# Full-width inverse steps, 33 weight columns, crossed decay sums and a new order in a fused RWKV-7 and SoLU kernel

## The chip, the cores and the metric

The kernel runs on one core of a Trainium2 chip. A core has five engines that run side by side, each its own instructions in order: TensorE (PE in the profile; its weight loads stand apart as PEld), VectorE (DVE), ScalarE (ACT), GpSimd (POOL) and SyncE (SP). SP, POOL and ACT also issue DMAs, which move data between DRAM and the on-chip memories. An instruction that needs another engine's result waits on a semaphore. The metric is the time of one execution on the device, in microseconds (us), as the median over several runs.

## What is computed

The first half is a recurrence with a 40 x 40 state for each of 4 batches and 8 heads over 768 steps; the second is a layer with a softmax gate and a norm over its outputs.

```python
for t in range(S):                      # S = 768, batch B = 4, heads H = 8, D = 40
    y[:, :, t] = einsum('bhd,bhde->bhe', r_t, state)
    Sa = einsum('bhde,bhe->bhd', state, a_t)
    state = state * w_t[:, :, None, :] - einsum('bhd,bhe->bhde', Sa, b_t) \
            + einsum('bhd,bhe->bhde', v_t, k_t)
x = y.transpose(0, 2, 1, 3).reshape(B * S, H * D)      # 3072 x 320
h = x @ w_in                                           # 320 x 1024
sm = softmax(h);  solu = h * sm
ln = (solu - mean) / sqrt(var + 1e-6) * g_ln
out = ln @ w_out                                       # 1024 x 320
```

All arithmetic is fp32. `w_in` and `w_out` lie in DRAM as float64; their words are taken apart on the chip and turned into fp32 ("narrowed").

## The kernel before

**Chunks.** The recurrence is cut into chunks of C = 64 steps. A chunk works on two of the four batches, one on partitions 0 to 63 and one on 64 to 127, so there are N = 24 chunks: even and odd ones alternate between the two batch pairs. Inside a chunk all is matrix products: `logged` takes the logarithm of w, a product with a triangle of ones sums it (`decay`, or `decay_by_halves` for chunks 12 to 23), the exponentials scale a and b (`aT`, `kb`), and the products of a with b give a strictly triangular 64 x 64 matrix for each head and batch (`norm`, kept negated as `nt`). The chunk's answer needs the inverse of one minus that matrix.

**The inverse.** Each 64 x 64 matrix is cut into 32 x 32 blocks (Q = 32). The two diagonal blocks of two chunks (one group n, 12 groups) are written to DRAM by `norm_stored`, read back by `spread` with one small matrix per partition (twice, the upper 64 partitions doing the other half of the columns), and inverted by forward substitution on VectorE (`invert`, lines 543 to 564): step j multiplies row j's factors into the columns done so far and adds. A step with fewer than four columns takes one fused instruction a column (L552); the others are cut into two parts, both products first (L560), then both sums (L563). The result goes to DRAM (`unloaded`) and comes back with `bring`: `tu` gets the block for the first 32 steps, `uh` that for the last 32. `flip` transposes the first; `couple` multiplies `nt`'s off-diagonal block with it, ScalarE brings the product to `wy` (L602), `close` multiplies that with `uh`, and ScalarE puts the result into the last columns of `tu` (L614). In `wy` the columns 32 to 63 hold an identity, so that close's product also copies `uh` itself into place; the factor `hi` zeroes the rows of the first 32 steps.

**The chunk's end.** `scores_k`, `scores_v`, `carried` and `driven` build the right side in `px`, ScalarE copies it to `x0`, `solved` multiplies with `tu`, `read` forms the answers, `answered` scales them, and `leave` and `left` turn them through DRAM into rows `xT` of the second half. Two chunks later (LAG = 2) `hidden` multiplies with `w_in` (five parts, H in the order), `highest`, `exped`, `weighed`, `spreadof` and `powered` do gate and norm, `folded` transposes, and `products_of` multiplies with `w_out`. The front of a chunk (loads, decays, `norm`) runs five chunks ahead (AHEAD = 5).

**Matmuls.** An fp32 matmul appears as two instructions in the trace. Operands of 64 rows and 64 columns use one quadrant of the array, so that four such products can run side by side; `in_turn` deals the units of work out over the quadrants.

**The order.** Every piece of work has a name: `i3.7` is step 7 of inverse 3, `Tc5` the decay sums of chunk 5 on PE and `xe5`, `xi5` their exponentials, `lg` the logarithm, `N`, `nt` the norm product and its copy, `sn` its way to DRAM, `Z`, `B`, `U` the clearing, loading and unloading of an inverse, `tu`, `uh` the loads of `bring`, `F`, `C`, `wy`, `D`, `tl` flip to close with their copies, `V`, `S`, `R0`, `R1` driven, solved and read, `nb`, `ns`, `nf` the three stages of narrowing a weight matrix part, and so on. The loops at the end of the function list the pieces in a default order; then all pieces named in the text `ORDER` (lines 31 to 74) come first, in the order written there, and the rest follow in the default order. Each engine and each DMA queue runs its pieces in that order and waits in line for what is not there yet. `ORDER` reaches to chunk 10; from there on the default loop sets the order: in it an h product group (`run(6)`) stands ahead of `couple`, another (`run(7)`) between `couple` and `close`.

## Time and profile before

| | |
|---|---|
| runs shown | 533.07, 534.18, 534.34 us; median 534.18 |
| the profiled execution | 535.16 us, of which 533.3 us are the span from the first to the last instruction |
| granted TensorE clock over the span | 0.99 |
| busy share of the span | PE 91%, PEld 74%, DVE 79%, ACT 59%, POOL 34% |
| the chain of work that ended last | PE 77%, DMA 8%, DVE 7%, ACT 3%, SP's queue 3%, issue 2% |
| `couple` (py<-tu,nt), 64 weight columns | 768 matmuls of 64x32, mean 223 ns each |
| `close` (py<-uh,wy), 64 weight columns | 768 matmuls of 64x32, mean 223 ns each |
| inverse steps on DVE | 576 products and 576 sums, mean 204 ns each; 144 fused ones, mean 242 ns |
| decay sums by halves (pst<-lw,cst) | 96 matmuls of 64x160, mean 309 ns each |

The profile is one execution, seen by the hardware profiler. "Busy" is the time in which an engine has an instruction in work; since instructions overlap in their pipelines, the mean duration of one is longer than the distance from one to the next. Times in a timeline or a chain are the start in us from the span's start, then the length. An instruction is named by engine, line (L552), operation and tiles (output<-inputs); "x12" is a count. The chain of waits follows the work back from the last instruction to what released it. A line that serves many callers (L318 is the matmul helper) is told apart by its tiles.

### The profile page before, as it was taken

What the parts mean: (1) busy time and instruction counts of PE and PEld (TensorE: products, weight loads), DVE (VectorE), ACT (ScalarE), POOL (GpSimd) and SP (SyncE); (2) the same over time, 40 slices, a digit from 0 to 9 for tenths busy, and PEclk for the clock granted to TensorE, in tenths of its full rate; (3) what the DMA queues carried; (4) which work ended last, traced back from release to release, by engine and by line L of the source; (5) the groups of instructions that cost most, each with busy time, mean ns of one, the idle gap of its engine ahead of it and who ended that gap; (6) DMA issues with size and microseconds to landing.
All of it is one profiled execution on the core that took longest, in us unless ns stands there. A gap on an engine that the chain in (4) does not pass through costs nothing.

```text
span 533.3 us, 28056 instructions
## 1 busy us (share of the span) xinstructions
PE 487.6 (91%) x12029; PEld 394.7 (74%) x12029; DVE 420.0 (79%) x1800; ACT 313.1 (59%) x627; POOL 180.2 (34%) x328
## 2 busy tenths in 40 slices
PE   4457589898999999999999999999999999999997
PEld 3345476666888877877888788788778877887766
DVE  5589988998998988879789879879979888544322
ACT  3546457785856655745766665566556655664433
POOL 3543237224434242533053343334252421210300
PEclk9999988998999999999999999999999999999999
DMA  9997679846666778766266675676554551420210
GB/s 155 171 185 149 150 140 187 189 95 118 133 134 129 131 154 142 150 142 141 48 135 117 124 163 100 116 152 123 105 120 95 109 115 43 103 68 27 62 53 25
DMA packets 194475, 63.95 MB, mean 120 GB/s; under 512 B 166840, under 2 KB 186528, under 8 KB 194352
## 3 DMA queue, kind: packets, MB, share of 16 engines
...
## 4 chain that ended last, share of the span: by engine, by line
PE 77%; DMA 8%; DVE 7%; ACT 3%; SPq 3%; issue 2%; DVEq 0%; ACTq 0%
PE po L318 19%; PE h L318 18%; PE py L318 6%; PE pyo L318 6%; PE px L318 6%; PE ps L318 4%; PE pu L318 3%; DMA a<-in_a_dram 3%; PE plnT L883 2%; PE pkv L435 2%; PE psr L318 2%; PE pb L435 2%; PE pa L435 2%; SPq L344 2%; DVE prod L560 1%
## 5 line engine op out<-in xcount | busy, mean ns | idle before, releaser
L318 PE MATMUL h<-w_in,xT 64*64 64x512 f32 (+1 forms) x1064 | 122.2, 551 | 0.4 <-issue 0.2
L318 PE MATMUL po<-w,lnT 128*128 128x160 f32 x768 | 114.7, 304 | 0.0
L318 PEld LDWEIGHTS po<-w,lnT 128*128 128x128 f32 x768 | 105.4, 190 | 4.6 <-issue 0.8
L560 DVE TENSOR_TENSOR prod<-blk,uu 128x48 f32<-128x48 f32 (+19 forms) x576 | 93.9, 204 | 1.2
L563 DVE TENSOR_TENSOR uu<-uu,prod 128x48 f32<-128x48 f32 (+19 forms) x576 | 94.2, 204 | 0.0
L525 POOL DMA_DIRECT2D nt_dram<-nt x86 | 50.1, 590 | 110.9 <-ACT nt L513 109.6
L318 PEld LDWEIGHTS h<-w_in,xT 64*64 64x64 f32 x1064 | 38.9, 133 | 24.9 <-issue 20.6
L834 DVE TENSOR_REDUCE nmax<-h 128x1 f32<-128x1024 f32 x24 | 29.3, 1221 | 32.1 <-PE h L318 31.5
L871 POOL TENSOR_TENSOR rs<-var,mhalf 128x1 f32<-128x1 f32 x24 | 13.7, 571 | 119.4 <-ACT var L863 119.1
L344 POOL DMA_DIRECT2D raw_r<-in_r_dram x48 | 33.0, 692 | 26.5 <-ACT r L379 24.5
L862 ACT ACTIVATE sq<-e,mu 128x1024 f32<-128x1024 f32 x24 | 26.9, 1120 | 19.9 <-DVE e L850 19.9
L479 DVE TENSOR_TENSOR lu<-pu,cst 128x512 f32<-128x512 f32 x24 | 16.5, 687 | 27.0 <-PE pu L318 27.0
L842 ACT ACTIVATE e<-h,nmax 128x1024 f32<-128x1024 f32 x24 | 26.7, 1110 | 17.5 <-DVE nmax L834 17.3
L850 DVE SCALAR_TENSOR_TENSOR e<-h,e 128x1024 f32<-128x1024 f32 x24 | 29.3, 1221 | 5.4 <-ACT e L842 5.2
L602 ACT ACTIVATE wy<-py,cst 128x256 f32<-128x256 f32 x24 | 11.4, 474 | 37.4 <-PE py L318 37.4
...
L552 DVE SCALAR_TENSOR_TENSOR uu<-blk,uu 128x30 f32<-128x30 f32 (+3 forms) x144 | 26.9, 242 | 2.5 <-DMA blk<-nt_dram 1.9
L665 ACT COPY st<-psr 128x416 f32<-128x416 f32 (+1 forms) x44 | 14.2, 377 | 24.7 <-PE psr L318 24.7
L629 ACT COPY kvT<-pkv 104x1024 f32<-104x1024 f32 x24 | 24.2, 1010 | 6.7 <-PE pkv L435 6.4
L318 PEld LDWEIGHTS py<-tu,nt 64*64 64x64 f32 x768 | 16.3, 141 | 14.2 <-issue 7.6
L318 PE MATMUL pu<-x,tu 64*64 64x104 f32 x768 | 25.9, 265 | 0.7 <-ACT bT L445 0.5
L318 PE MATMUL px<-lv,psi 64*64 64x104 f32 x768 | 24.2, 264 | 2.2 <-DVE lv L479 2.2
...
## 6 DMA issues: line engine op xcount, KB each, us to landing
...
```

Source lines behind the costliest of these rows:

```text
L318: nc.tensor.matmul(o, lhsT=lhsT, rhs=rhs, start=start, stop=stop, skip_group_check=True)
L344: queue.dma_start(out=x[half(p), :, 0:D], in_=ap[2 * bp + p, :, ci * C:(ci + 1) * C, :].rearrange("h t d -> t h d"))
L435: nc.tensor.transpose(out=t[0:W2, p, at + C * j:at + C * j + C], in_=x[half(p), 2 * j:2 * j + 2].rearrange("p a b -> p (a b)")[:, skip:ski ...
L525: queue.dma_start(out=blocks[n][e].rearrange("(a x h) s c -> a x s h c", a=GRP, x=2)[at, x], in_=nt[home:home + Q].rearrange("p h j c -> p ...
L552: nc.vector.scalar_tensor_tensor(out=u[:, c, j + 1:Q], in0=nb[:, j, j + 1:Q], scalar=u[:, c, j:j + 1], in1=u[:, c, j + 1:Q], op0=ALU.mult, ...
L560: nc.vector.tensor_tensor(out=ts[-1], in0=nb[:, j:j + 1, j + 1:Q].to_broadcast([P, hi - lo, m]), in1=u[:, lo:hi, j:j + 1].to_broadcast([P, ...
L563: nc.vector.tensor_tensor(out=u[:, lo:hi, j + 1:Q], in0=u[:, lo:hi, j + 1:Q], in1=x, op=ALU.add)
L629: return lambda: nc.scalar.copy(out=o[0:W2].rearrange("p b j t -> p b (j t)"), in_=t[0:W2])
L834: nc.vector.tensor_reduce(out=nmax, in_=d["h"], axis=AX.X, op=ALU.max, negate=True)
L842: nc.scalar.activation(out=e, in_=d["h"], func=AF.Exp, bias=d["nmax"], accum_out=d["esum"])
L850: nc.vector.scalar_tensor_tensor(out=d["e"], in0=d["h"], scalar=1.0 / DFF, in1=d["e"], op0=ALU.mult, op1=ALU.mult, accum_out=d["mu"])
L862: nc.scalar.activation(out=pair("A" if i == N - 2 else "h", "sq").rearrange("p a b -> p (a b)"), in_=d["e"], func=AF.Square, scale=-float( ...
```

## The change

1. **Full-width steps.** For the first six inverses (`WIDE = 6`) a step with one column stays one fused instruction; every other step becomes one product over all its columns and one sum. Each is a piece of its own: the product keeps the name `i3.7`, the sum is `j3.7`, so other work can be put between them. Inverses 6 to 11 keep the old steps.
2. **33 weight columns.** `couple` uses the last 33 of `nt`'s 64 columns as weights, `close` 33 rows and 33 columns of `wy`. The first of the 33 meets a row of zeros. `wy` has 33 columns, the last of them zero; the identity and the factor `hi` leave the constants table. The block that the identity used to copy now comes by two DMAs of its own (`ut`, on SP) into `tu`, and `uh` holds half as many heads. The copies to `wy` and into `tu` are two ScalarE instructions each, one for each half of the partitions.
3. **Crossed decay sums.** From chunk index 12 (the 13th chunk) on, `logged` writes the second half of the heads' logarithms to the other 64 partitions, in three instructions in place of one, and the four products of `decay_by_halves` lie on four quadrants of the array in place of two.
4. **Order.** `ORDER` is new throughout and reaches to chunk 12. In the default loop `couple` stands ahead of the h group of `run(6)`.
5. The load of `g_ln` moves from ScalarE's queue to GpSimd's.

```diff
@@ -24,53 +24,72 @@
 LAG = 2
 EARLY = 10
 NK = 5
+NARROW = Q + 1
+WIDE = 6
 FIRST = 6
+CROSSED = EARLY + 2
 SPLITS = {2: (0, 0, 0, 2, 4), 24: (0, 0, 0, 0, 2)}
-w0 b0 b1 w1 a0 lg0 Tc0 xi0 xe0 Tei0 sb0 Tb0 Ta0 L1 lg1 Tc1 Eei0 Ea0 v0 Eb0 xi1 xe1 N0 nt0 Tei1 Eei1 sb1 Tb1 a1 Ta1 Ea1
-L0 Eb1 N1 nt1 w2 lg2 a2 Tc2 nb0 k0 Z0 sn0 nb1 ns1 nf1 sn1q sk0 ns0 nf0 sn1 w3 xe2 b2 Z1 Ta2 xi2 B0 Tei2 Eei2 r0 Ea2
...
+w0 b0 b1 lg0 Tc0 xi0 xe0 sb0 w1 K1 lg1 Tc1 xi1 sb1 Tei0 a0 Eei0 Ta0 Ea0 L0 a1 w2 Tb0 xe1 Tei1 Eb0 N0 k0 k1 sk0 nt0 Tb1
+Ta1 k2 b2 Eei1 Ea1 Eb1 N1 Z0 nb0 L1 lg2 nt1 r0 cr0 Tc2 xe2 Tei2 xi2 sb2 nb1 ns1 nf1 sk1 b3 sk2 sn0 sn1q sn1 w3 lg3 Tb2
+B0 i0.1 Tc3 Eei2 xi3 i0.2 b4 b5 i0.3 a2 xe3 j0.3 i0.4 j0.4 i0.5 j0.5 i0.6 j0.6 i0.7 j0.7 Eb2 g Ta2 Ea2 N2 i0.8 j0.8
+i0.9 j0.9 i0.10 ns0 Z1 v0 r1 sb3 j0.10 i0.11 j0.11 w4 lg4 Tc4 a3 nt2 a4 i0.12 j0.12 i0.13 w5 Tei3 Eei3 j0.13 i0.14
...
 """
 LN_EXP = "natural_log_exp_and_others"
@@ -84,8 +103,6 @@
         ident=np.eye(P),
         cum=same & (s <= t),
         tri=row < np.arange(C)[None, :],
-        eye_hi=row == Q + np.arange(Q)[None, :],
-        hi=(row >= Q).astype(np.float64),
         mean=np.full((P, P), 2.0 ** -10),
     )
     at, where = 0, {}
@@ -173,11 +190,10 @@
     r_t = zeroed(nc.gpsimd, "r", [P, H, C], 1, pad)
     st_t = zeroed(nc.vector, "st", [P, 2, 8, C], NPAIR)
     tu_t = zeroed(nc.vector, "tu", [P, H, 3 * Q], 2)
-    uh_t = zeroed(nc.vector, "uh", [P, 2 * H, Q], 2)
+    uh_t = zeroed(nc.vector, "uh", [P, H, Q], 2)
     x0 = const.tile([P, 2, 4, W2], FP32, name="x0")
-    wy = const.tile([P, 2, 4, C], FP32, name="wy")
-    nc.vector.tensor_copy(out=wy.rearrange("p h j c -> p (h j) c")[:, :, Q:],
-                          in_=c_("eye_hi").unsqueeze(1).to_broadcast([P, 8, Q]))
+    wy = const.tile([P, 2, 4, NARROW], FP32, name="wy")
+    nc.vector.memset(wy[:, :, :, Q:], 0.0)
     above = const.tile([C, Q // 2, Q], FP32, name="above")
     nc.gpsimd.memset(above, 1.0)
     for x in range(Q // 2):
@@ -381,7 +397,13 @@
     def logged(i):
         lw = st[i]["lw"] = two.tile([P, DM], FP32, tag="lw", name="lw", bufs=1)
-        nc.scalar.activation(out=lw, in_=st[i]["raw_w"].rearrange("p h d -> p (h d)"), func=AF.Ln)
+        raw = st[i]["raw_w"].rearrange("p h d -> p (h d)")
+        if i < CROSSED:
+            nc.scalar.activation(out=lw, in_=raw, func=AF.Ln)
+            return
+        nc.scalar.activation(out=lw[:, 0:DM // 2], in_=raw[:, 0:DM // 2], func=AF.Ln)
+        for p in range(2):
+            nc.scalar.activation(out=lw[half(1 - p), DM // 2:], in_=raw[half(p), DM // 2:], func=AF.Ln)
     def decay(i, t=None):
         if not ok(i):
@@ -407,7 +429,8 @@
         t = t[:, :, 256:256 + width]
         for x in range(2):
             for p in range(2):
-                mm(t[half(p), x], c_("cum")[half(p), half(p)], d["lw"][half(p), width * x:width * x + width])
+                y = half(p ^ x)
+                mm(t[half(p), x], c_("cum")[y, y], d["lw"][y, width * x:width * x + width])
         def evict():
             nc.scalar.activation(out=ei_t[0].rearrange("p (x h) d -> p x h d", x=2)[:, :, :, 0:D],
@@ -545,6 +568,22 @@
         flat = u.rearrange("p c t -> p (c t)")
         nc.vector.tensor_tensor(out=u[0:C], in0=nb[0:C, 0::2], in1=above, op=ALU.mult)
         nc.vector.memset(flat[0:C, 0::Q + 2], 1.0)
+        for j in range(1, (Q - 1) * (n < WIDE)):
+            m, n_c = Q - 1 - j, (j + 1) // 2
+            if n_c == 1:
+                nc.vector.scalar_tensor_tensor(out=u[:, 0, j + 1:Q], in0=nb[:, j, j + 1:Q], scalar=u[:, 0, j:j + 1],
+                                               in1=u[:, 0, j + 1:Q], op0=ALU.mult, op1=ALU.add)
+                yield
+                continue
+            prod = two.tile([P, P], FP32, tag=f"wide{n % 2}", name=f"wide{n % 2}", bufs=1)[:, 0:n_c * m]
+            x = prod.rearrange("p (c r) -> p c r", c=n_c)
+            nc.vector.tensor_tensor(out=x, in0=nb[:, j:j + 1, j + 1:Q].to_broadcast([P, n_c, m]),
+                                    in1=u[:, 0:n_c, j:j + 1].to_broadcast([P, n_c, m]), op=ALU.mult)
+            yield
+            nc.vector.tensor_tensor(out=u[:, 0:n_c, j + 1:Q], in0=u[:, 0:n_c, j + 1:Q], in1=x, op=ALU.add)
+            yield
+        if n < WIDE:
+            return
         for j in range(1, Q - 1):
             m, n_c = Q - 1 - j, (j + 1) // 2
             if n_c < 4:
@@ -581,7 +620,10 @@
             queue = nc.sync if i or not x else nc.gpsimd
             queue.dma_start(out=d["tu"][C * x:C * x + Q, :, Q:2 * Q], in_=src[0, at, :, x])
         for x in range(2 * (which == "u")):
-            nc.sync.dma_start(out=d["uh"][C * x + Q:C * x + C], in_=src[1, at].rearrange("c x h t -> c (x h) t"))
+            nc.sync.dma_start(out=d["uh"][C * x + 1:C * x + 1 + Q].rearrange("c (x h) t -> c x h t", x=2),
+                              in_=src[1, at][:, :, 4 * x:4 * x + 4])
+        for x in range(2 * (which == "v")):
+            nc.sync.dma_start(out=d["tu"][C * x + Q:C * x + C, :, 2 * Q:], in_=src[1, at, :, x])
     def flip(i):
         if not ok(i):
@@ -598,9 +640,13 @@
             p, q, g, h = u
             j = 2 * q + g
             x = half(p ^ h)
-            mm(t[half(p), h, j * Q:j * Q + Q], d["nt"][x, p, j], d["tu"][x, 4 * p + j, 0:Q])
-        return lambda: nc.scalar.activation(out=wy[:, :, :, 0:Q], in_=t[:, :, 0:4 * Q].rearrange("p h (j c) -> p h j c", j=4),
-                             func=AF.Copy, scale=c_("hi"))
+            mm(t[C * p:C * p + NARROW, h, j * Q:j * Q + Q], d["nt"][x, p, j, C - NARROW:], d["tu"][x, 4 * p + j, 0:Q])
+
+        def evict():
+            for p in range(2):
+                at = slice(C * p, C * p + NARROW)
+                nc.scalar.copy(out=wy[at, :, :, 0:Q], in_=t[at, :, 0:4 * Q].rearrange("p h (j c) -> p h j c", j=4))
+        return evict
     def close(i):
         if not ok(i):
@@ -610,9 +656,15 @@
         for u in in_turn(lambda p, q, g, h: (p, p ^ h)):
             p, q, g, h = u
             j = 2 * q + g
-            mm(t[half(p ^ h), p, 384 + j * Q:384 + j * Q + Q], wy[half(p), h, j], d["uh"][half(p), H * (p ^ h) + 4 * p + j])
-        return lambda: nc.scalar.copy(out=d["tu"].rearrange("p (h j) c -> p h j c", h=2)[:, :, :, 2 * Q:],
-                       in_=t[:, :, 384:].rearrange("p h (j c) -> p h j c", j=4))
+            y, z = p ^ h, slice(C * p, C * p + NARROW)
+            mm(t[C * y:C * y + NARROW, p, 384 + j * Q:384 + j * Q + Q], wy[z, h, j], d["uh"][z, 4 * y + j])
+
+        def evict():
+            for y in range(2):
+                at = slice(C * y, C * y + Q)
+                nc.scalar.copy(out=d["tu"][at].rearrange("p (h j) c -> p h j c", h=2)[:, :, :, 2 * Q:],
+                               in_=t[at, :, 384:].rearrange("p h (j c) -> p h j c", j=4))
+        return evict
     def attend_kv(i, t, which):
@@ -949,7 +1001,7 @@
     def stepped(n):
         if n not in stepping:
             stepping[n] = invert(n)
-        next(stepping[n])
+        next(stepping[n], None)
     def lazily(tag, name):
         box = []
@@ -964,6 +1016,8 @@
         while due and due[0][0] <= last and n:
             x, left_ = due[0]
             do(f"i{x}.{Q - 1 - left_}", stepped, x)
+            if x < WIDE and Q - 1 - left_ > 2:
+                do(f"j{x}.{Q - 1 - left_}", stepped, x)
             n -= 1
             due[0][1] -= 1
             if not due[0][1]:
@@ -1041,6 +1095,7 @@
         if ok(i):
             do(f"tu{i}", bring, i, "t")
             do(f"uh{i}", bring, i, "u")
+            do(f"ut{i}", bring, i, "v")
     def xy(i):
         return "BC" if i < EARLY - AHEAD else ("BC", "CB")[(i - EARLY + AHEAD) % 2]
@@ -1053,7 +1108,7 @@
         keys(i, "w")
         keys(i, "b", nc.scalar)
         keys(i, "a")
-    do("g", lambda: nc.scalar.dma_start(out=g_rows, in_=moe_g_ln.rearrange("(c p) -> c p", p=P)))
+    do("g", lambda: nc.gpsimd.dma_start(out=g_rows, in_=moe_g_ln.rearrange("(c p) -> c p", p=P)))
     logged_(0)
     keys(2, "w")
     for n in range(2):
@@ -1290,9 +1345,9 @@
         ahead = 2 + (i >= EARLY - AHEAD)
         logged_(j + ahead)
         vector(plan[2], i)
-        run(6)
         if ok(i + 1):
             evict(f"wy{i + 1}", do_pe(f"C{i + 1}", lambda i=i: couple(i + 1)))
+        run(6)
         if i == LAG + 1:
             do("centre", lambda: centred(mean["mean2"]))
         run(7)
```

94 lines of the change are left out of this document (54 added, 40 removed).

## The prediction

> **What bounds the kernel now.** I read the page's totals and slices first, then the windows by stage, then the chain of waits and the timelines of PE and DVE inside the stages.
>
> ```profile
> span 533.3 us, 28056 instructions
> PE 487.6 (91%) x12029; PEld 394.7 (74%) x12029; DVE 420.0 (79%) x1800; ACT 313.1 (59%) x627; POOL 180.2 (34%) x328
> PE   4457589898999999999999999999999999999997
> DVE  5589988998998988879789879879979888544322
> 0.00:29.40 29.40, 13.33 (x152) 10.29 (x152) 15.36 (x41) 14.08 (x27) 13.51 (x47) 1.00 0.95 161
> 29.40:168.20 138.80, 116.45 (x2893) 92.90 (x2897) 130.65 (x606) 89.07 (x184) 55.11 (x92) 0.96 0.74 147
> 168.20:260.00 91.80, 89.57 (x2308) 74.45 (x2302) 77.75 (x339) 52.82 (x107) 32.18 (x55) 1.00 0.70 137
> 260.00:520.00 260.00, 258.90 (x6612) 208.28 (x6607) 193.50 (x816) 152.27 (x299) 78.88 (x135) 1.00 0.48 100
> ```
>
> The columns of a window are its length, then the busy time of PE, PEld, DVE, ACT and POOL. There are two regimes. From 29.4 us (first step of inverse 0) to 168.2 us (flip of chunk 6) DVE is busy 130.65 of 138.80 us and PE idles 22.35: VectorE sets the pace. From 260 us on PE is busy 258.90 of 260: what leaves PE's path there leaves the end, one for one. Between them PE loses 2.2 us. So each part of the change must be priced in the regime in which it lies: DVE work before chunk 6 delays the moment from which PE runs full; PE work saved before that moment only becomes idle time; PE work saved behind it is a gain.
>
> **Part 1: full-width steps, inverses 0 to 5.** The costs are on DVE.
>
> ```profile
> 22.31 0.69 DVE L251 SCALAR_TENSOR_TENSOR w<-w,scale 128x512 int32<-128x512 int32 x1
> 22.91 0.69 DVE L252 SCALAR_TENSOR_TENSOR w_in<-w,w_in 128x512 f32<-128x512 uint16 x1
> 23.63 0.69 DVE L253 TENSOR_TENSOR w_in<-w_in,w 128x512 f32<-128x512 f32 x1
> 24.24 0.68 DVE L462 TENSOR_TENSOR aT<-pa,ex 104x512 f32<-104x512 f32 x1
> 29.40 2.23 DVE L552 SCALAR_TENSOR_TENSOR uu<-blk,uu 128x30 f32<-128x30 f32 x12
> 31.55 0.33 DVE L560 TENSOR_TENSOR prod<-blk,uu 128x48 f32<-128x48 f32 x2
> ...
> 35.79 0.48 DVE L428 TENSOR_TENSOR kb<-raw_b,inv 128x320 f32<-128x320 f32 x1
> 36.19 0.35 DVE L560 TENSOR_TENSOR prod<-blk,uu 128x64 f32<-128x64 f32 x2
> ...
> 44.76 0.27 DVE L560 TENSOR_TENSOR prod<-blk,uu 128x7 f32<-128x7 f32 x2
> 44.96 0.27 DVE L563 TENSOR_TENSOR uu<-uu,prod 128x7 f32<-128x7 f32 x2
> 45.15 0.69 DVE L462 TENSOR_TENSOR aT<-pb,ex 104x512 f32<-104x512 f32 x1
> ```
>
> Whether an instruction uses the result of the one just ahead of it decides. L252 does not use L251's result and starts 0.60 us behind it, though L251 lasts 0.69: neighbours overlap. L253 uses L252's and starts 0.72 behind: it waits the full duration and 0.03 more. The old step hides that wait: two products, then two sums, each input two instructions old, and the last pair of 7 elements costs 0.20 us for two, the duration of one (0.171 below) and 0.03. The full-width step is one product and one sum, each using the result just ahead, and the next product uses the sum. Where nothing stands between, each of its instructions costs its whole duration and 0.03.
>
> ```profile
> L560 DVE TENSOR_TENSOR prod<-blk,uu 128x72 f32<-128x72 f32 x12 | 2.7, 227 | 0.0
> L560 DVE TENSOR_TENSOR prod<-blk,uu 128x7 f32<-128x7 f32 x12 | 2.1, 171 | 0.0
> L782 DVE TENSOR_TENSOR st<-tot,ex 104x160 f32<-104x160 f32 x40 | 11.1, 320 | 0.1
> ```
>
> Step j has (31-j) rows and half of j+1 columns; the 28 wide steps (j = 3 to 30) hold 2,541 elements, 91 on the average. From 72 to 160 elements the duration grows by 1.06 ns an element, so 91 take 0.247. The 56 instructions cost 56 x 0.277 = 15.5 us, and two single-column steps 0.5: 16.0 an inverse. Before, inverse 0 took 2.15 (L552 x12) and 13.6 from 31.55 to 45.15, less the 1.4 of two key scalings (0.40 each, as from 35.79 to 36.19) and one aT product (0.60) inside it: 14.35. **So DVE pays 1.65 us more an inverse**, with half the instructions. The other bound is no wait at all: 0.07 + 1.04 ns x 91 an instruction (0.60 for 512 elements above, less 0.53), 9.7 us an inverse, 4.65 less. I take the dear one: two rows show the wait, none shows a dependent neighbour without it.
>
> The Trainium skill speaks the other way: "VectorE: DVE Perf Modes", in its rules for kernel authors, says of chained operations that the count of instructions is what to minimize. By that rule halving the count would be the gain of the cheap bound; the 0.20 for a pair above shows that the old form has already hidden most of what the rule wants saved.
>
> **Part 2: the new order.** I counted the named DVE pieces between the first step of inverse 0 and the flip of chunk 6 in both lists. Before: 128 steps (inverses 0 to 3 and 8 of inverse 4); after: 130, one aT product more, one end of a weight split (L251 to L253) more, two key scalings fewer; all other kinds agree. At 0.51 a step (12.2 / 24), 0.60, 1.93 (22.31 to 24.24) and 0.40 that is 1.0 + 0.6 + 1.9 - 0.8 = 2.7 us more. With four inverses of part 1 (6.6) **9.3 us more DVE work stands ahead of flip 6.** The start doesn't move: inverse 0 hangs on chunk 1's a, nt and two DMA trips in both lists.
>
> ```profile
> 168.16 0.44 DVE L590 STREAM_TRANSPOSE tu<-tu 128x256 f32<-128x256 f32 x1
> 169.53 0.66 PE L318 MATMUL py<-tu,nt 64*64 64x32 f32 x31
> 297.55 0.91 SPq L584 DMA_DIRECT2D uh<-uu_dram  x2
> ```
>
> Flip 6 ends at 168.60, its couple starts at 169.53: 0.9 of cover. DVE had 8.15 us idle in that stretch; with more queued ahead some of it goes, between 0 and 8, and I take 3. PE's own 2.2 us of loss after chunk 6 overlap the slip: 1. The change adds two inverse loads a chunk on SP (0.91 as uh's pair), behind which key loads queue; early, where SP issues almost without a gap, I charge 1 us for all (0 to 3). **Slip: 9.3 - 0.9 - 3 - 1 + 1 = +5.4** (bounds 0 and 12.7, the latter under the second rival).
>
> **Part 3: 33 weight columns.**
>
> ```profile
> 286.14 0.86 PE h L318 x8
> 287.00 0.44 PE py L318 x32
> 287.44 0.89 PE h L318 x8
> 288.33 0.44 PE py L318 x31
> 288.77 0.74 PE px L318 x32
> ...
> 297.32 0.55 PE pst L318 x5
> ...
> 298.73 0.93 PE ps L318 x64
> ```
>
> This is the chain of waits inside one steady chunk, all PE: start, time, group. Thirty-two matmuls on four quadrants are 8 deep. px streams 104 columns: 0.74 / 8 = 92 ns, 0.89 a column. ps streams 64: 58 ns, 0.91. Couple and close (py, 0.44 each) stream only 32 and take 55 ns, as long as 64 columns: what is 64 there is the weights. If the weight columns set it, 33 take 8 x 33 x 0.87 = 0.23, and each group saves 0.21. If something else holds a short matmul at 55 ns, it saves 0. No row has few columns on both sides; I take 0.21, since the time per weight column (0.86) meets the time per streamed column. Chunks 7 to 23 lie behind the slip: **17 x 2 x 0.21 = 7.1 us** (0 to 7.1). Chunks 0 to 6 gain nothing that lasts.
>
> ACT pays for it.
>
> ```profile
> 281.24 0.47 ACT L413 ACTIVATE ei<-pst 128x320 f32<-128x320 f32 x1
> 281.57 0.47 ACT L418 ACTIVATE inv<-pst 128x320 f32<-128x320 f32 x1
> 287.52 0.47 ACT L602 ACTIVATE wy<-py,cst 128x256 f32<-128x256 f32 x1 [1.05 <-PE py L318]
> 288.85 0.37 ACT L614 COPY tu<-py 128x256 f32<-128x256 f32 x1 [0.86 <-PE py L318]
> 298.32 1.03 ACT L888 COPY lnT<-plnT 128x1024 f32<-128x1024 f32 x1
> 299.48 1.47 PE L318 MATMUL h<-w_in,xT 64*64 64x512 f32 x12
> ```
>
> wy and tl become two copies each. Neighbours follow after their elements' time (0.33 for 320), so 256 follow after 0.27: the pair takes 0.64, which is 0.17 more for wy and 0.27 more for tl. Close waits for wy; before, one h group (0.89) covered that, and the couple now stands ahead of two (0.86 + 0.89), so 0.64 and the semaphore fit; without that cover it would be 0.2 a chunk. Behind tl wait x0 and the exponential on ACT. ACT is busy 152 of 260 us, and tl itself is used a chunk later: nothing. The smaller table, the cleared column of wy and g's load (one issue, moved from ACT's queue to POOL's, which is busy 34%) cost nothing that PE meets; their bound is 0.5 us.
>
> **Part 4: decay sums in four quadrants.** Eight matmuls of 160 columns sit on two quadrants, 4 deep: 4 x 160 x 0.87 = 0.56, as the 0.55 shows. On four they are 2 deep: 0.28 less. But the next h waits for lnT, which ends at 299.35 against h's start at 299.48, and lnT's start doesn't depend on these sums: 0.13 of room is sure, up to 0.28 where lnT is earlier. I take 0.15. Chunks 14 to 23 have it behind the slip: **1.5 us** (1.3 to 2.8). The logarithm goes from one ACT instruction to three of half the width: 3 x 0.17 and a tail, 0.2 to 0.4 more, off the path for the same reason as tl.
>
> **The sum.** +5.4 - 7.1 - 1.5 = **-3.2 us**. Against the profiled execution (535.16 us, of which 533.3 are the span and 1.9 lie around it) that gives 532.0; the median of the runs shown is 1.0 below that execution, so I predict **531.0 us**.
>
> **The rivals.**
>
> *A. A floor under short matmuls (slower).* What couple and close meet is a least time of 55 ns a matmul, not the weights. For it: 64 x 64 and 64 x 32 differ by under 0.03 us a group. Against it: nothing in the trace but the agreement per weight column. Then part 3 gives nothing: 5.4 - 1.5 = +3.9, **538.1 us**. It decides as soon as the slip exceeds 1.5. The Trainium skill has such a rule: "TensorEngine Tiling (Array Packing)", on instruction overhead, says that a matmul pays some 60 cycles and that one with a single column takes as long as one with 60. By that rule couple and close stay as they are.
>
> *B. DVE stays the bound up to chunk 8 (slower).* Inverses 4 and 5 pay 3.3 us more and no idle time of DVE is taken back: 9.3 + 3.3 - 0.9 + 1 = 12.7 of slip; the savings count from chunk 9 on, 15 x 2 x 0.21 + 1.5 = 7.8: +4.9, **539.1 us**. For it: DVE is busy 77.75 of 91.80 us from 168 to 260 too, and 9.3 us more are carried into it. Against it: the 14 us that it idled there.
>
> *C. No wait inside the wide step (much faster).* Then four inverses save 18.6, and flip 6 comes up to 15.9 earlier. PE had 22.35 us idle in that stretch, and perhaps half of the 15.9 and the DMA trips between can be had, some 10: with 8.6 behind it, **515.6 us**. Against it stand 0.72 and 0.20 above.
>
> **How the numbers follow.** Forecast 0.53, A 0.20, B 0.17, C 0.10. 0.3% is 1.6 us, about what a measurement of this kernel tells from no change. The forecast's own range is 527 to 536, so of its 0.53 I give 0.38 to faster, 0.12 to the same, 0.03 to slower. A and B give 0.32 to slower and 0.05 to the same; C is faster. That makes 0.48, 0.17, 0.35. The range 522 to 541 holds the forecast, A and B with room for the worse bound of the slip (12.7 without the cheaper weights, less 1.5, would be 545, left out) and for the best case of slip 0 (524); it leaves out C.
>
> **What would show each step.** Dependent TENSOR_TENSORs of some 120 elements spaced near 0.31 us and wide inverses near 16 us show part 1 right; spacings near 0.2 show C. Flip 6 near 174 us and PE idle of some 27 us before it show the slip; flip 6 near 168 would say that DVE's idle took it all. py groups of 0.23 in the chain of waits show part 3; 0.44 shows A. A pst group of 0.28 with h waiting for lnT shows part 4. The prediction fails if py stays at 0.44, or if chunk 8 is late by over 8 us.

## The result, and the profile after

| | before | after |
|---|---|---|
| median of the runs | 533.62 us (529.09 to 535.81, 6 runs) | 549.02 us (546.63 to 555.81, 6 runs) |
| ratio of the runs, 95% interval | | 1.030 (1.023 to 1.037) |
| the profiled execution, and its span | 535.16, 533.3 us | 547.21, 545.1 us |
| flip of chunk 6 | 168.16 us | 174.54 us |
| hidden-layer maximum of chunk 9 | 288.85 us | 299.78 us |
| the same of chunk 22 | 509.97 us | 522.09 us |

The change makes the kernel 3% slower. Now and then an execution of one and the same kernel runs over 1.5% slower than its fastest; the ratios leave such executions out and the medians do not, so a ratio need not be the quotient of two medians. The page's totals and slices after:

```profile
span 545.1 us, 27948 instructions
PE 484.3 (89%) x12029; PEld 387.4 (71%) x12029; DVE 415.8 (76%) x1500; ACT 334.9 (61%) x699; POOL 181.9 (33%) x329
PE   4456487889999989979999999999999999999997
PE 69%; DVE 10%; DMA 7%; SPq 6%; issue 4%; ACT 4%; POOL 0%; DVEq 0%; POOLq 0%; ACTq 0%
```

PE has 3.3 us less to do (484.3 against 487.6), in the direction that the narrower weights should bring, and DVE 300 instructions less. But the chain that ended last now lies on PE for 69% and no longer for 77%: more of the span hangs on DVE, on SP's queue and on waits. The windows by stage, cut as before (length, then PE, PEld, DVE, ACT, POOL busy, the granted clock, DMA):

```profile
29.40:168.20 138.80, 108.81 (x2749) 86.64 (x2753) 125.37 (x384) 90.91 (x191) 50.76 (x84) 0.98 0.78 144
168.20:260.00 91.80, 84.24 (x2290) 66.99 (x2283) 72.25 (x234) 56.95 (x125) 29.98 (x52) 0.98 0.67 129
260.00:520.00 260.00, 256.87 (x6667) 207.13 (x6663) 199.08 (x838) 164.90 (x341) 82.11 (x138) 1.00 0.50 101
```

Before, PE was busy 89.57 of 91.80 us in the middle window; now 84.24, and also 84.24 when a window of that length starts at the new kernel's own flip 6 (174.54). That window, in which the forecast had PE full again, loses 5.3 us. In the last one PE idles 3.1 us where it idled 1.1. The starts in the table's last rows say the same: 6.4 us late at flip 6, 10.9 at chunk 9, 12.1 at chunk 22. The forecast was +5.4, +5.4 (less the first savings) and -3.2.

Two places stand out in the trace. The first: ScalarE's timeline, then one row each of SP's and PE's, from 230 us:

```profile
231.01 0.45 ACT L794 COPY lu<-pu 128x320 f32<-128x320 f32 x1
237.07 0.46 ACT L395 COPY v<-lv 128x320 f32<-128x320 f32 x1 [5.62 <-DMA lv<-in_v_dram]
237.44 0.59 ACT L536 ACTIVATE nt<-py 128x512 f32<-128x512 f32 x1
...
232.83 0.62 SPq L360 DMA_DIRECT2D lv<-in_v_dram  x1
...
238.08 0.45 PE L334 MATMUL py<-tu,nt 64*33 64x32 f32 x23 [3.05 <-ACT nt L536]
```

The new order puts ScalarE's copy of chunk 10's values (`cv10`) two places behind the load that brings them (`v10`); in the old list it stands 44 places behind it. The load goes out at 232.83, ScalarE stands until 237.07, the eviction `nt` of chunk 13 stands behind it, and PE's couple of chunk 9 behind that: 3.05 us of idle PE in the PE-bound part. The next view is the windows around it:

```profile
235.00:238.00 3.00, 0.03 (x3) 0.00 (x0) 1.85 (x4) 0.93 (x2) 0.00 (x0) 1.00 0.76 122
238.00:241.00 3.00, 2.92 (x84) 2.21 (x88) 0.50 (x1) 0.79 (x4) 2.33 (x4) 0.54 0.62 101
241.00:242.00 1.00, 1.00 (x34) 0.87 (x26) 0.73 (x1) 0.69 (x2) 0.00 (x0) 0.66 0.43 63
```

When PE starts again its granted clock is 0.54, then 0.66: 3 x 0.46 + 0.34 = 1.7 us more. This stall costs its own length and then 1.7 us. It is the only one of PE's stalls between flip 6 and chunk 9 with a slow clock behind it; the next longest, 1.60 us before 196.63, has none. The second place is in the steady part, in the chain of waits of the new kernel:

```profile
426.41 0.28 PE py L334 x29
426.69 1.77 PE h L334 x15
428.46 0.30 PE py L334 x25
428.76 0.79 PE px L334 x32
...
438.53 0.86 PE h L334 x6
439.39 0.59 issue
439.98 1.13 PE h L334 x9
```

The couple takes 0.28 and the close 0.30 where both took 0.44; yet an h group is now interrupted by 0.59 us of "issue", which the kernel before has nowhere in this stretch. What the two places are worth at the end is for the experiments to say.

### The profile page after: what moved, and what is told of

Its sections match the earlier page's. It is cut to its first block, busy times and chain, and to the rows that moved or that the text cites. A ratio compares the mean times of both kernels' runs of the same rounds, so it can differ in the third digit from the quotient of the medians.

```text
span 545.1 us, 27948 instructions
## 1 busy us (share of the span) xinstructions
PE 484.3 (89%) x12029; PEld 387.4 (71%) x12029; DVE 415.8 (76%) x1500; ACT 334.9 (61%) x699; POOL 181.9 (33%) x329
## 4 chain that ended last, share of the span: by engine, by line
PE 69%; DVE 10%; DMA 7%; SPq 6%; issue 4%; ACT 4%; POOL 0%; DVEq 0%; POOLq 0%; ACTq 0%
PE po L334 19%; PE h L334 18%; PE pyo L334 6%; PE px L334 5%; PE py L334 4%; PE ps L334 4%; SPq L360 4%; PE pu L334 3%; DVE wide L580 2%; DVE uu L583 2%; PE plnT L935 2%; PE pkv L458 2%; PE pa L458 2%; PE psr L334 2%; DMA raw_w<-in_w_dram 1%
## 5 line engine op out<-in xcount | busy, mean ns | idle before, releaser
L334 PEld LDWEIGHTS h<-w_in,xT 64*64 64x64 f32 x1064 | 42.1, 135 | 38.7 <-issue 35.8
L923 POOL TENSOR_TENSOR rs<-var,mhalf 128x1 f32<-128x1 f32 x24 | 16.3, 678 | 100.4 <-ACT var L915 99.9
L599 DVE TENSOR_TENSOR prod<-blk,uu 128x60 f32<-128x60 f32 (+28 forms) x288 | 46.7, 202 | 0.6
L602 DVE TENSOR_TENSOR uu<-uu,prod 128x60 f32<-128x60 f32 (+28 forms) x288 | 46.8, 202 | 0.0
L583 DVE TENSOR_TENSOR uu<-uu,wide 128x110 f32<-128x110 f32 (+19 forms) x168 | 42.2, 251 | 4.7
L580 DVE TENSOR_TENSOR wide<-blk,uu 128x110 f32<-128x110 f32 (+19 forms) x168 | 42.1, 251 | 4.5
L665 ACT COPY tu<-py 32x256 f32<-32x256 f32 x48 | 17.4, 362 | 31.7 <-PE py L334 28.3
L360 POOL DMA_DIRECT2D raw_r<-in_r_dram x48 | 33.0, 693 | 11.6 <-ACT r L395 11.3
L854 POOL DMA_DIRECT2D x_dram<-x x24 | 17.2, 718 | 51.0 <-DVE x L845 38.5
L648 ACT COPY wy<-py 33x256 f32<-33x256 f32 x48 | 17.5, 365 | 26.4 <-PE py L334 26.2
L502 DVE TENSOR_TENSOR lu<-pu,cst 128x512 f32<-128x512 f32 x24 | 16.5, 688 | 22.5 <-PE pu L334 21.4
L823 DVE TENSOR_TENSOR tot<-pyo,st 104x416 f32<-104x416 f32 x44 | 24.1, 582 | 5.5 <-PE pyo L334 5.4
```

The costliest lines, as they stand in the source:

```text
L334: nc.tensor.matmul(o, lhsT=lhsT, rhs=rhs, start=start, stop=stop, skip_group_check=True)
L360: queue.dma_start(out=x[half(p), :, 0:D], in_=ap[2 * bp + p, :, ci * C:(ci + 1) * C, :].rearrange("h t d -> t h d"))
L580: nc.vector.tensor_tensor(out=x, in0=nb[:, j:j + 1, j + 1:Q].to_broadcast([P, n_c, m]), in1=u[:, 0:n_c, j:j + 1].to_broadcast([P, n_c, m]) ...
L583: nc.vector.tensor_tensor(out=u[:, 0:n_c, j + 1:Q], in0=u[:, 0:n_c, j + 1:Q], in1=x, op=ALU.add)
L599: nc.vector.tensor_tensor(out=ts[-1], in0=nb[:, j:j + 1, j + 1:Q].to_broadcast([P, hi - lo, m]), in1=u[:, lo:hi, j:j + 1].to_broadcast([P, ...
L602: nc.vector.tensor_tensor(out=u[:, lo:hi, j + 1:Q], in0=u[:, lo:hi, j + 1:Q], in1=x, op=ALU.add)
```

## The experiments

Each kernel ran beside the kernel before on the same chip; its own median moved between 528.3 and 532.9 us from chip to chip, so the ratios are compared.

| kernel | median, us | ratio to the kernel before, 95% interval |
|---|---|---|
| the new kernel once more (after_again) | 544.27 | 1.023 (1.015 to 1.032) |
| new order alone (order_alone) | 539.97 | 1.019 (1.013 to 1.026) |
| 33 columns alone (cols_alone) | 536.68 | 1.011 (1.004 to 1.019) |
| full-width steps alone (wide_alone) | 532.91 | 1.006 (1.002 to 1.010) |
| decay sums alone (decay_alone) | 527.85 | 1.002 (0.998 to 1.005) |
| new kernel with old steps (no_wide) | 544.80 | 1.030 (1.024 to 1.036) |
| new kernel with 64 columns (no_cols) | 542.31 | 1.026 (1.021 to 1.031) |
| new kernel, cv10 moved (late_cv10) | 542.79 | 1.029 (1.026 to 1.032) |
| old order to flip 6, then new (old_then_new) | 541.15 | 1.013 (1.004 to 1.022) |
| new order to flip 6, then old (new_then_old) | 536.71 | 1.009 (1.003 to 1.014) |
| 33 columns, ut9 moved (cols_ut9) | 535.28 | 1.015 (1.012 to 1.017) |
| added loads only (spare_loads) | 537.86 | 1.014 (1.007 to 1.021) |
| split copies only (split_copies) | 536.80 | 1.011 (1.003 to 1.019) |
| 33 columns, two h groups (cols_two_groups) | 536.83 | 1.009 (1.003 to 1.015) |
| 33 columns, loads on POOL (cols_pool) | 537.67 | 1.011 (1.005 to 1.017) |
| 33 columns from chunk 11 on (late_cols) | 533.43 | 1.001 (0.997 to 1.004) |

**A second profile of the kernel before** (before_again), no edit.

> The kernel before, one more profile, to see where its executions of 525 us differ from the profiled one of 533. All theories: 525 to 534 us; if the clock is the difference, the stretches at half clock at 76 to 83 and 128 to 131 us are missing where it is short.

Measured: 527.2 us, span 525.3. The profile of the prediction had PE at a granted clock of 0.50 to 0.71 from 76.4 to 83 us and 0.50 from 127.7 to 131; this one has 1.00 throughout, and its maximum of chunk 0 starts at 96.97 instead of 100.82. From chunk 5 on the prediction's profile lies 6 to 8 us behind it; about 5 of these are the two stretches at half clock (6.8 and 3.4 us), the rest is not explained. The second profile is the better base for what follows, though it lies 2.3 us under the median of its chip (529.49). Flip 6 is the flip of chunk 6. The table gives the start of flip 6 and of the hidden layer's maximum (one instruction a chunk on DVE), minus its start in this second profile, in us:

| | flip 6 | chunk 0 | 3 | 5 | 6 | 9 | 15 | 22 |
|---|---|---|---|---|---|---|---|---|
| before, second profile, start | 163.42 | 96.97 | 165.12 | 204.49 | 227.01 | 282.59 | 393.71 | 502.02 |
| before, first profile | 4.7 | 3.8 | 4.7 | 6.1 | 6.2 | 6.3 | 7.3 | 8.0 |
| after | 11.1 | 10.1 | 12.8 | 11.5 | 13.5 | 17.2 | 17.5 | 20.1 |
| after_again | 9.0 | 7.9 | 11.6 | 10.2 | 11.6 | 14.8 | 15.0 | 16.5 |
| order_alone | 8.8 | 9.7 | 11.0 | 8.2 | 9.0 | 12.8 | 12.9 | 13.4 |
| no_wide | 7.4 | 7.5 | 11.0 | 9.1 | 13.3 | 16.6 | 17.8 | 20.0 |
| wide_alone | 6.5 | 5.3 | 5.4 | 8.2 | 6.0 | 6.6 | 7.1 | 7.1 |
| cols_ut9 | 2.2 | 1.3 | 2.7 | 4.0 | 7.1 | 7.0 | 6.5 | 6.2 |
| spare_loads | 2.2 | 2.6 | 2.4 | 4.5 | 7.2 | 7.2 | 8.5 | 8.8 |
| split_copies | 2.7 | 3.4 | 2.7 | 3.0 | 2.9 | 4.1 | 6.4 | 9.3 |

Single profiles carry some us of clock ahead of chunk 4, as the second row shows; what grows behind chunk 5 is safer to read. The rows of the new kernel and of order_alone show two steps, one up to flip 6 and one between chunks 5 and 9; the order by itself has most of both.

**Each part alone.** The order without the rest:

```diff
 ORDER = """            # before
-w0 b0 b1 w1 a0 lg0 Tc0 xi0 ...
+w0 b0 b1 lg0 Tc0 xi0 xe0 sb0 w1 ...       # the new text; names j and ut unused
-    do("g", lambda: nc.scalar.dma_start(...
+    do("g", lambda: nc.gpsimd.dma_start(...
     # default loop: run(6) behind couple, as in the change
```

> The old kernel in the new order: old inverse steps (a step of inverses 0 to 5 stands where its first half stands), 64 weight columns, old decay sums; the load of g goes to POOL as in the new kernel. Theory 1 (the inverses' longer steps are the loss): the order only puts 2.7 us more DVE work ahead of flip 6, so 534 to 537 us, flip 6 at 168 to 171. Theory 2 (the narrow columns' extra loads and copies are the loss): 533 to 535 us. Theory 3 (the order itself is the loss: it starves PE between chunks 6 and 10 by asking for inverse 5's load late): at least 541 us, with PE idle for 3 us or more between 190 and 260 us.

Measured 1.019, some 10 us: theory 3. PE idles 3.55 of the 70 us from 190 to 260, 2.26 of them before 234.32 as in the new kernel. The windows from the first step of inverse 0 to flip 6, of the kernel before (second profile) and then of this one:

```profile
27.74:163.42 135.68, 112.39 (x2893) 89.86 (x2893) 130.21 (x604) 88.88 (x184) 54.66 (x92) 1.00 0.76 151
```

```profile
29.46:172.23 142.77, 116.00 (x2946) 92.37 (x2949) 133.68 (x614) 89.19 (x183) 49.80 (x84) 0.99 0.77 145
```

DVE has 3.5 us more to do ahead of flip 6 (the prediction counted 2.7), idles 9.1 us instead of 5.5, and inverse 0 starts 1.7 us later: these are the 8.8 us of the table. The other profiles bear out the work and soften the rest. With the old list up to flip 6 and the old steps (eleven profiles) DVE is busy for 130.0 to 130.7 us there and idle for 5.5 to 10.6, and flip 6 comes at 163.4 to 168.9; with the new list and the old steps (three profiles) it is busy for 133.4 to 133.7 and idle for 8.1 to 9.1, and flip 6 comes at 170.9 to 172.2. So the order adds 3 us of work and takes back no idle time that these profiles show.

The columns without the rest:

```diff
+names ut{i} right behind uh{i} in the old ORDER; NARROW, bring, couple and close as in the change
```

> 33 weight columns alone, in the old order, each chunk's second inverse load right behind its first; old steps, old decay sums. Theory 1 and theory 3: the groups of couple and close go from 0.44 to about 0.29 us, 0.15 us x 2 x 17 chunks behind chunk 6 = 5 us less, 528 to 530 us. Theory 2: what the matmuls save is given back by the added loads and the split copies, 533 to 540 us.

Measured 1.011, 6 us slower, so theory 2's sign. The steps without the rest:

```diff
+            prod = two.tile([P, P], FP32, tag="wide", ...)     # one scratch tile
 in the old ORDER: i3.7 -> i3.7 j3.7, for inverses 0 to 5
```

> Full-width steps for inverses 0 to 5 alone, in the old order, each step's sum right behind its product; both inverses' products share one scratch tile instead of alternating between two. 64 weight columns, old decay sums. Theory 1: 1.65 us more an inverse, four of them ahead of flip 6 and two more up to chunk 8, less 0.9 of cover and some idle time: 537 to 543 us, flip 6 at 170 to 174. Theories 2 and 3: 533 to 536 us.

Measured 1.006, 3.2 us, just under theory 1, which begins at 3.4 (537 against 533.6 in the first comparison). Flip 0 stands behind inverse 0 alone; its row in the second profile of the kernel before, and in this one:

```profile
59.60 0.43 DVE L590 STREAM_TRANSPOSE tu<-tu 128x256 f32<-128x256 f32 x1
```

```profile
61.24 0.43 DVE L608 STREAM_TRANSPOSE tu<-tu 128x256 f32<-128x256 f32 x1
```

Of these 1.64 us, 0.49 are a later start of the inverse (28.23 for 27.74). A better measure is the time that DVE gives to the inverse: for each of its instructions, from the end of DVE's instruction ahead of it to its own end, without waits of over 0.1 us. For inverses 0 to 3 together that is 66.0 us here and 59.6 in the second profile, 1.6 us more an inverse; the prediction's price was 1.65. In the new order it is another matter: 62.3 us in the new kernel (62.2 in after_again) against 58.9 in order_alone, 0.85 us more an inverse. There other pieces of work stand between products and sums, above all in inverses 1 and 2. Flip 6, behind four inverses, is 6.5 us late in wide_alone (169.91 against 163.42; 1.5 us of that may be a stretch at a clock of 0.61 near 106 us).

The decay sums without the rest:

```diff
+CROSSED, logged and decay_by_halves as in the change; old ORDER
```

> The new decay sums alone in the old order (chunks 14 to 23 with 64 columns and old steps). As predicted: 0.15 us less in each of 10 chunks, 1 to 1.5 us less than before. Rival (the split logarithm on ScalarE delays lnT, for which the next hidden-layer group waits): 0 to 3 us more.

Measured 1.002 (0.998 to 1.005): nothing that can be told, against 1.5 us less. The trace says why, further down.

**All but one part.**

```diff
-        for j in range(1, (Q - 1) * (n < WIDE)):       # no_wide: the new steps and the names j left out
...                        # no_cols: couple, close, bring and wy as before; one scratch tile, not two
```

> The new kernel with the old inverse steps throughout (new order, 33 weight columns, new decay sums). Theory 1: 6.6 to 9.9 us less than the new kernel, 538 to 542 us. Theory 2: 546 to 549 us. Theory 3: still at least 541 us, with the same idle time of PE between chunks 6 and 10.

> The new kernel with 64 weight columns (new order, wide steps with one scratch tile, new decay sums). Theory 3 alone: as the order alone, plus nothing for the steps and 0 to 1 us less for the decay sums, 538 to 541 us, and no issue gaps in the hidden layer's matmuls near 440 and 475 us if these come from the columns' small loads. Rival (the new kernel's loss is its steps, or the decay sums): 545 us or more.

Measured 1.030 and 1.026, against 1.023 to 1.030 for the whole. Beside the new order the steps cost nothing that can be told at the end, and the columns do not repay anything either. The parts alone sum to 3.8%, more than the whole. The table shows one place where delays do not add: no_wide has its flip 6 1.6 and 3.7 us ahead of the two profiles with the new steps, but then PE stands 5.01 us before chunk 9's couple (3.05 and 2.71 with the new steps), 6.8 us at half clock go with it (3.4), and by chunk 6 the lead is gone. no_cols is above the 538 to 541 that theory 3 expected; the issue gaps of the h groups near 440 and 475 us (1.16 and 0.87 in no_wide) are gone in it, but its chunks there are still 0.3 to 0.6 us longer than those of order_alone.

**The order: one name, and two halves.**

```diff
-mlu8 cv10 w17 Z6 ... C9 t0.8 t1.8 an8 H6.4 m6 wy9 D9 tl9 rs5
+mlu8 w17 Z6 ... C9 t0.8 t1.8 an8 H6.4 m6 wy9 D9 tl9 cv10 rs5
```

> The new kernel with one name of its order moved: cv10, ScalarE's copy of chunk 10's values, goes from two places behind their load (v10) to behind chunk 9's close (tl9), where nothing waits behind it. Theory 3 (the order): ScalarE no longer stands 5.6 us before that copy with the eviction nt and chunk 9's couple behind it, so PE's stall of 3.0 us before 238 us goes, and with it the stretch at 0.78 of the clock behind it (1.7 us): 3.5 to 5 us less than the new kernel, about 544 to 546 us. Rival (the loads come late as such and PE only waits at the next place): at most 1 us less, 548 to 550 us.

> The new kernel unchanged, so that it, its parts and the kernel before stand on one chip. All theories: 1.03 times the kernel before, 542 to 546 us where the kernel before takes 528. If moving cv10 was worth the 4.3 us by which the two profiled spans differ, it lies 3 us or more above late_cv10's 542.8; if not, within 1.5 us of it.

The wait ahead of the couple falls from 3.05 (2.71 in the second profile of the new kernel) to 1.53 us and the slow clock behind it goes; the maximum of chunk 6 starts at 237.86 instead of 240.50 (238.64 in the second profile of the new kernel). The medians, 542.79 and 544.27 on one chip, lie within the 1.5 us that were set as the sign of no gain, and the ratios, 1.029 and 1.023, show none. The chain in the trace is real, but at the end it is not worth its 4.7 us: the rival holds better than the theory.

```diff
 old_then_new: names of the old ORDER up to F6, then what is left in the new order
 new_then_old: names of the new ORDER up to F6, then what is left in the old order; g on GpSimd
 both: the default loop as before
```

> The kernel before (old steps, 64 columns, old decay sums) with the old order for all pieces up to the flip of chunk 6, and the new order for what is left. Theory 6 (most of the order's loss of 10 us arises ahead of flip 6, where it gives DVE 5 us more to do and 4 us more to wait for): flip 6 at 163 to 168 us as in the old order, and 2 to 5 us above the kernel before at the end, from chunk 10's values (cv10) on. Rival 7 (the loss sits in the new order behind chunk 6): 8 us or more above it.

> The kernel before with the new order for all pieces up to the flip of chunk 6, and the old order for what is left. Theory 6: flip 6 at 171 to 175 us, and 6 to 9 us above the kernel before at the end. Rival 7: at most 3 us above it.

(The 5 us more to do in the first of these expectations came of a window that begins 1.6 us behind inverse 0's first step in the second profile; from that step on they are 3.5, as above.) Measured 1.013 and 1.009, together about the 1.019 of the whole order: neither theory 6 nor rival 7, both halves cost. Flip 6 comes at 171.1 in new_then_old. In old_then_new it comes at 168.8, and nearly 7 us are lost between the maxima of chunks 2 and 3 (153.7 to 177.4 us; 148.05 to 165.12 before), at full clock and around the joint at flip 6, where pieces that the new order had already done are still due; that these are the reason is not shown. So the cut says that the old arrangement around flip 6 cannot be had by halves, but not which pieces of the new list are to blame.

**The columns: loads or copies.**

```diff
-... Eei14 uh9 ut9 v10 Er9 Tc15 xi15 Es9 xe15 lg16 l6
+... Eei14 uh9 v10 Er9 Tc15 xi15 Es9 xe15 lg16 l6 ut9
```

> 33 weight columns alone in the old order, with one name moved: chunk 9's second inverse load (ut9) goes from ahead of v10 and the xT load behind them on SP's queue to behind that xT load. Theory 4 (in the old order the columns lose by what the added load delays on SP): the hidden layer's wait of 3.5 us for xT at 221 us, the 2.6 us behind it at 246 and the slow clock behind both go, and the columns' 0.3 us a chunk shows at the end: 524 to 529 us, faster than the kernel before by 0.3 to 1%. Rival (the added loads and the split copies cost it everywhere): 533 us or more, as with the columns alone.

Measured 1.015: no better than without the move, so moving one load behind xT is not enough; PE still waits 1.25 us for xT at 220.00. Then each side effect by itself, with 64 columns:

```diff
+    spare = const.tile([P, H, Q // 2], FP32, name="spare")               # spare_loads
+        for x in range(2 * (which == "v")):
+            nc.sync.dma_start(out=spare[C * x + Q:C * x + C], in_=src[1, at, :, x, :, 0:Q // 2])
-        return lambda: nc.scalar.activation(out=wy[:, :, :, 0:Q], ...    # split_copies
+            for p in range(2): nc.scalar.activation(out=wy[half(p), :, :, 0:Q], ...
-        return lambda: nc.scalar.copy(out=d["tu"] ...
+            for y in range(2): nc.scalar.copy(out=d["tu"][half(y)] ...
```

> The kernel before with the second inverse load of the 33-column form added and nothing else: the same 512 pieces a chunk from the inverse in DRAM, on SP's queue right behind the first, at half the bytes (64 a piece), into a spare tile that nobody reads. Theory 4 (the columns lose by the added loads): most of the 6 to 8 us that separate the columns from the kernel before, so 532 to 536 us against 528. Rival 5 (they lose by the split copies on ScalarE): 527 to 530 us.

> The kernel before with the evictions of couple and close split into two by partitions, as the 33-column form does, and nothing else. Rival 5: close waits for the second copy in every early chunk and ScalarE falls behind, 532 to 536 us. Theory 4: 527 to 530 us; as predicted, the copies are hidden.

Measured 1.014 and 1.011: each of the two alone costs about what the columns cost (their intervals overlap, so they cannot be ranked). The loads first: SP's and PE's rows for chunk 6's hidden layer, in the second profile of the kernel before and then with the spare loads.

```profile
210.38 1.24 SPq L812 DMA_DIRECT2D xT<-x_dram  x2
...
215.81 0.65 PE L318 MATMUL h<-w_in,xT 64*64 64x512 f32 x3 [0.51 <-DMA xT<-x_dram]
```

```profile
217.97 0.58 SPq L815 DMA_DIRECT2D xT<-x_dram  x1
...
221.54 1.04 PE L319 MATMUL h<-w_in,xT 64*64 64x512 f32 x2 [2.87 <-DMA xT<-x_dram]
```

From 196 to 218 us SP issues almost without a gap (loads of w, v, a, k, b, an output, `uh`, and xT at the end). Before, xT goes out 5.9 us after the maximum of chunk 5 and PE still waits 0.51 us for it: there is no slack. With two more pairs of 0.93 in that queue it goes out 9.0 us after, PE waits 2.87, and its clock is 0.69 in the 4 us from 224: in the table the lateness goes from 4.5 to 7.2 between chunks 5 and 6. cols_ut9 has one of the two pairs left ahead of xT and loses 3.1 there.

The copies cost in the other part. The close's group from 300 to 490 us, split copies and then the kernel before (idle before it at the end):

```profile
L318 PE MATMUL py<-uh,wy 64*64 64x32 f32 x352 | 7.4, 222 | 2.1 <-ACT wy L605 2.1
```

```profile
L318 PE MATMUL py<-uh,wy 64*64 64x32 f32 x352 | 7.0, 216 | 0.0
```

In the default order one h group (0.89) stands between couple and close, and it doesn't cover two copies: the close starts 1.25 us behind the start of that group and no longer 0.89 (0.19 of it is shown as a wait), and a chunk without front work takes 17.37 us instead of 16.96. This 0.4 us is the price of these copies, not of the change's: the two copies of 64 x 256 take 0.95 us together, those of 33 x 256 in the 33-column kernels 0.74, and their couple ends 0.16 us sooner. In cols_ut9, with one h group as cover, no close behind chunk 0 waits over 0.05 us for `wy`, and the period is 16.85.

```diff
-        run(6)
         if ok(i + 1):
             evict(f"wy{i + 1}", do_pe(f"C{i + 1}", ...
+        run(6)                                              # cols_two_groups: cols_ut9 with this
-            nc.sync.dma_start(out=d["tu"][C * x + Q:C * x + C, :, 2 * Q:], ...
+            nc.gpsimd.dma_start(...                         # cols_pool: cols_alone with both
```

> 33 weight columns in the old order with ut9 behind the xT load, as before, and from the first chunk that the written order doesn't name the couple one hidden-layer group earlier, so that two groups and not one lie between couple and close (as in the new kernel). Theory 8 (behind chunk 9 the columns' gain of 0.33 us a chunk goes into close's wait for wy's two copies): the period of a chunk without front work goes from 16.84 to 16.65 us, 2 us less than the columns with ut9 moved, 532 to 534 us where the kernel before takes 528.5. Rival (the gain is lost to something else): the period stays at 16.8 us or more, 534 to 536 us.

> 33 weight columns in the old order with the couple earlier in the steady chunks as in the run above, and the second inverse load issued on POOL's queue and not on SP's. Theory 4 (the loads lose by their place on SP, where every issue ahead of chunk 8's xT counts): without them there the hidden layer doesn't wait for xT at 220 us, nothing runs at half clock behind it, and the columns gain what they save: 521 to 526 us, faster than the kernel before by 0.5 to 1.4%. Rival (the loads cost by their pieces on the DMA engines or by POOL's own queue, wherever they are issued): 530 us or more.

With two h groups the period goes from 16.85 (mean of chunks 16 to 19, cols_ut9) to 16.76: theory 8's direction, at half its size. Over the chunks behind the written order that is 1 us; the ratios, 1.015 and 1.009 on two chips, have intervals that overlap. With the loads on POOL the hidden layer no longer waits at 220 us, and chunk 9 is 3.8 us late in place of 7.0; but 1.011 is the rival's. POOL's, ScalarE's and PE's rows show one place where it goes:

```profile
277.86 1.23 POOL L586 DMA_DIRECT2D tu<-uu_dram  x2 [3.69 <-PE pu L317]
...
285.21 1.36 POOL L343 DMA_DIRECT2D raw_r<-in_r_dram  x2
...
286.14 0.46 ACT L378 COPY r<-raw_r 128x320 f32<-128x320 f32 x1 [3.19 <-DMA raw_r<-in_r_dram]
286.51 0.47 ACT L383 ACTIVATE lw<-raw_w 128x320 f32<-128x320 f32 x1
286.88 0.73 ACT L608 COPY wy<-py 33x256 f32<-33x256 f32 x2
...
287.66 0.46 PE L317 MATMUL py<-uh,wy 33*33 33x32 f32 x32 [2.21 <-ACT wy L608]
```

The load waits on POOL until PE has read the old `tu` (3.69), the load of r behind it lands late, ScalarE's copy of r stands 3.19 us with wy behind it, and close waits 2.21. Here the delay has only changed its queue. This stall takes chunk 10 from 3.8 to 7.0 us late; by chunk 22 it is 12.5, and what adds the rest was not followed.

```diff
+NARROW_FROM = 11
+            if i < NARROW_FROM: ...       # bring, couple and close as before; else the 33-column form
```

> The kernel before with 33 weight columns from chunk 11 on only, where PE is the bound and the written order has ended: there the couple stands ahead of two hidden-layer groups and the second inverse load goes on SP right behind the first; chunks 0 to 10 as before. Theory (the columns' own price is right where copies and loads are hidden, and their loss lies in the early chunks): up to chunk 10 as the kernel before, then 0.2 to 0.3 us less a chunk, 2 to 4 us less in all, ratio 0.993 to 0.997. Rival (the added load and copies eat it in the chunks with front work too): ratio 0.998 to 1.004.

Measured 1.001 (0.997 to 1.004): the rival. Where such a saving can go shows in the periods of single chunks. In the second profile of the new kernel those of chunks 17 and 19 are 16.73 and 16.70 us (16.96 before), those of chunks 16 and 18 are 18.58 and 17.63; the profile of late_cols has 18.10 and 18.32 in these two, at full clock. The chain shown above has such a place, 0.59 of issue at 439.39 inside an h group (a part only of the 1.4 us by which chunk 16 is longer there); SP's rows beside it:

```profile
437.02 2.01 SPq L621 DMA_DIRECT2D tu<-uu_dram  x2
439.09 0.91 SPq L623 DMA_DIRECT2D uh<-uu_dram  x2
440.05 0.92 SPq L626 DMA_DIRECT2D tu<-uu_dram  x2
```

The gap comes while the inverse loads go out. That they cause it isn't shown: spare_loads, with as many pieces, keeps 16.96 to 16.98 in these chunks, and so do order_alone and wide_alone; cols_two_groups, with the same loads and the same place for the couple, has 16.68 to 16.88; no_cols, without the narrow loads, has 17.60 and 17.25 in chunks 16 and 17. None of the versions beats the kernel before.

## Why the prediction was wrong, step by step

The forecast was 532.0 us for the profiled pair; 547.2 came. By the starts of the table in the section on the result the 15.2 us are 1.0 up to flip 6 (6.4 late instead of 5.4), 4.5 from there to chunk 9, 8.6 of savings that were to come and did not, and 1.2 that grew instead. The step that failed first is the price of the new order in the slip; the second is the saving of part 3.

- **The two regimes** were right: DVE busy up to chunk 6, PE from 260 us on.
- **Part 1, the price of a wide step, was right where nothing stands between its instructions.** Neighbours in DVE's timeline of the new kernel:

```profile
212.54 0.28 DVE L580 TENSOR_TENSOR wide<-blk,uu 128x120 f32<-128x120 f32 x1
212.85 0.28 DVE L583 TENSOR_TENSOR uu<-uu,wide 128x120 f32<-128x120 f32 x1
213.17 0.28 DVE L580 TENSOR_TENSOR wide<-blk,uu 128x114 f32<-128x114 f32 x1
```

Spaced 0.31, duration and 0.03, as forecast, and 1.6 us more an inverse in wide_alone. The sum, though, charged it to all four inverses ahead of flip 6 (6.6 us); in the new order DVE gives them 3.4 us more. Rival C is out, and with it the rule of the Trainium skill's page "VectorE: DVE Perf Modes" in its rules for kernel authors, that the number of instructions is what to minimize: here the number fell from 1800 to 1500 on DVE and the inverses took longer.

- **Part 2 failed: the order.** With its 2.7 us of work, the 0.9 of cover, the 3 of idle time taken back and the 1 of PE's loss, the slip made the order by itself a gain of 2.2 us, and behind flip 6 it charged nothing. The count of the work was about right (3 us more in all the profiles). The credit for idle time and the sentence "The start doesn't move" were not: order_alone idles 3.6 us more than the second profile of the kernel before, starts inverse 0 1.7 us later, has flip 6 8.8 us late and 4.0 us more between there and chunk 9, and costs 1.9%. Its two halves cost 1.3% and 0.9%. The loads, ScalarE's copies and POOL's queue of the new list were not followed at all; cv10 is one place where this shows, and moving it repaired that place but not the time. That flip 6 came 6.4 us late where 5.4 were forecast is luck: the kernel before had itself lost 4.7 us up to there in the profile that was read, and against its second profile the slip is 11.1 and 9.0 us.
- **Part 3 failed in two terms, and one held.** The groups take 0.28 and 0.30 in the chain, so each saves 0.15 and not 0.21; and the h groups and px beside them take up some of that: from the end of pyo to the next pyo the steady chunk goes from 3.37 to 3.13 us, and its period from 16.96 to 16.73. 17 x 0.23 = 3.9 us would be left, not 7.1, and no kernel with the columns shows even that at the end. "1 us for all" of SP's added loads is 7 us in the old order (spare_loads, 1.014): the sum knew the 0.91 of a pair, and did not see that xT, at the end of that queue, had no slack. What the loads cost beside the new order is not shown; no_cols says only that columns and loads together gain nothing there. "ACT extra hidden" held in the new kernel: behind flip 6 no close waits for `wy` in either of its profiles.
- **Part 4** was right about its matmuls, but not about the gain. The chain from the decay group to the next h group, in the kernel before (second profile) and then in the new one:

```profile
272.62 0.55 PE pst L318 x5
273.17 0.02 PE pu L318 x2
273.19 0.08 PE pst L318
273.27 0.76 PE pu L318 x28
274.02 0.93 PE ps L318 x64
```

```profile
327.63 0.43 PE pst L334 x8
328.06 0.71 PE pu L334 x32
328.77 0.02 issue
328.79 1.16 PE ps L334 x64
```

The decay group takes 0.43 for 0.63, 0.20 less where 0.28 was worked out, but ps then takes 1.16 for 0.93, and h starts 2.33 us behind the first decay sum where it was 2.34. decay_alone has the same 0.43, 1.16 and 2.33. So the saving of 0.15 a chunk was not there, and not because of lnT; why ps takes longer is open.

- **The rivals.** A and B had the right side, at 538 and 539 us. A's mechanism is refuted by the trace (0.44 became 0.28). B's is too: DVE idles 19.2 of the 91.8 us behind the new kernel's flip 6. No rival had the loss where it was: the order's delay up to flip 6, and PE's stalls between chunks 6 and 9, the longest of them with a slow clock behind it.
- **The base.** The profile that was read held 10.2 us at half clock, which cost 5.1 us. The 8.15 us of DVE's idle time, of which 3 were to be taken back, are 5.5 in the second profile.

What stays open: which pieces of the new list cost the 1.9%, what eats the columns' saving where copies and loads are covered, and what stretches single h groups in chunks 16 to 19 of the new kernel.
